# Gram inputs and key-query tiles in two transfers of 48 partitions each, in a delta-rule attention and two-MLP kernel

## The chip, the cores and the metric

The kernel runs on one core of a Trainium2 chip. The metric is the device time of one execution in microseconds (us); lower is better. The core has engines that work side by side, each through its own list of instructions in order: PE (matrix multiply; its weight loads are shown apart as PEld), DVE (vector), ACT (scalar functions), POOL (GpSimd) and SP, which here only issues transfers between HBM and on-chip memory. On-chip memory (SBUF) has 128 partitions.

## What is computed

A linear attention with a delta-rule state over 768 tokens for 4 x 8 heads of width 48, then an ELU MLP, then an MLP with a rational activation; cut from the reference:

```python
    k_n = k / (np.linalg.norm(k, axis=-1, keepdims=True) + 1e-06)
    for t in range(S):
        y[:, :, t] = np.einsum('bhd,bhde->bhe', q[:, :, t], state)
        v_old = np.einsum('bhde,bhd->bhe', state, kt)
        state = state + bt[:, :, :, None] * np.einsum('bhd,bhe->bhde', kt, vt - v_old)
...
    h = x @ w_in                                  # 3072 x 384 by 384 x 2048
    g = np.where(h > 0.0, h, alpha * (np.exp(np.minimum(h, 0.0)) - 1.0))
    return (g @ w_out).astype(np.float32)
...
    g = P / (Q + 1e-06)                           # second MLP: cubic over quadratic in h
    return (g @ w_out).astype(np.float32)
```

## The kernel before

The 768 tokens are cut into 12 chunks of 64 (`s`), two chunks to a window (`w`, six windows of 512 rows for the MLPs). A chunk's 32 heads lie in two halves (`hf`); in a half's tile, each of two heads-in-a-partition-column (`h`) has its 48 features at partitions 64h to 64h+47.

**Gram stage** (`g_item`): per chunk, two groups of 32 small matmuls (64 records in the trace, two for each) multiply keys by keys and queries. Its inputs are tiles of 128 x 1024 floats, `c_kg`, one for each chunk and half, loaded by `gin_ahead` into `wo`, `xg` or `gin` (the first six are parked in memory that other tiles use later; the name in the trace is that of the memory). `layout` on the host fills partitions 48 to 63 and 112 to 127 of these tiles with zeros; the matmuls read only the 48 rows of a head. **Solve stage** (`t_pieces`): the Gram blocks are transposed on DVE (`am<-gl_`) and a triangular system is inverted by a chain of DVE products and sums, in which ACT moves blocks (`tt<-tt`, `am<-tt`); it ends with the transpose `tp_t<-am`. **Chain stage** (`chain`): per chunk `ks`, two solves (`pa<-kv,tp_t` or `pa<-R,tp_t`), `lo`, `yy`, `xx`, `ku` on PE with DVE and ACT between them. It reads tiles `kq` (`c_kq`, the same shape and the same zero rows as `c_kg`) and `kv`. **MLP 1** (`H`, `A1`, `B1`, `C1`, `O`): matmuls of 512 columns, in groups of nine, between which the small groups of the next windows are put. **MLP 2** follows from about 560 us.

Weights arrive as 64-bit floats and are converted on ACT and DVE (`conv_x`, `conv_d`, `conv_s`; tiles `raw`, `ce`, `wo`, `wi`).

What sets the order: every operation is recorded first, and `order` plans all engines by a model of the chip (`simulate`, `backward`); ties and small shifts come from a table of random seeds (`MIX`), and `PUSH` gives the settings of successive passes, of which the best is kept. All instructions are then emitted at one line (L206). `gaps` puts dummy matmuls named `fill` (line 1629) in front of a small group where the plan leaves PE idle, only for groups planned after 20 us. SP issues its transfers in the order planned; eight completion semaphores are used in turn, so a transfer waits in SP's queue until the one eight before it has landed. `hold(t)` is a one-column copy on POOL into a tile that keeps its load from being issued before an event (the first mask, the first transpose); `follow(t, u)` does the same until tile `u` has landed.

At the start PE runs three warm-up matmuls on zeros (`pa<-tmp`), then four Gram groups for window 0. The first two use the first two `c_kg` tiles, the third and fourth the next two (`wo`, `xg`). Behind these in SP's queue are `mask_p`, `beta_l`, two `raw<-w_out`, two tiny coefficient loads, two `kv` and eight `wo<-w_in`; then, after the first transpose, the loads for window 1.

Of the kernel before, what the change touches and what calls it, by code (L numbers as in the profile page):

```python
# [20 lines left out]
D = 48  # L21
NSC = 12
# [164 lines left out]
class Recorder:  # L187
# [141 lines left out]
SLACK = {"small": 150, "F": 100, "x": 30, "issue": 450, "rate": 385, "land": 2300, "wait": 900, "space": 3500, "room": 264, "first": 460, "blk": 253.9, "use": 2250, "hold": 400, "jit": 300, "keep": 6000, "most": 5000, "step": 3500, "drift": 0,  "pj": 0}  # L329
MIX = [  # L330
# [4 lines left out]
]  # L335


PUSH = [(16000, 5000), (5000, 3000), (16000, 3000), (0, 3000), (20000, 3000), (13000, 3000), (0, 500), (18000, 3000)]


def draw(seed, n):
# [13 lines left out]
def order(ops):  # L355
# [30 lines left out]
    best = None  # L386
    for push, lead in PUSH:
        end = simulate(ops)
# [235 lines left out]
def kernel(  # L624
# [16 lines left out]
    rc = Recorder(nc)  # L641
    mm, act, vector, gpsimd = rc.mm, rc.act, Recorder.Eng(rc, "DVE", nc.vector), Recorder.Eng(rc, "POOL", nc.gpsimd)
# [74 lines left out]
    def hold(t):  # L717
        gpsimd.tensor_copy(out=t[:, 0, 0:1], in_=gate[-1])

    def follow(t, u):  # L720
        gpsimd.tensor_copy(out=t[:, 0, 0:1], in_=u[:, 0, 0:1])

    conv_q = []
    for f in range(NF):
# [82 lines left out]
    def gin_park(i):  # L807
        if i < 3:
            return wo1.rearrange("p f n -> p (f n)")[:, 1024 * i:1024 * i + 1024]
        if i == 3:  # L810
            t = ap1.tile([128, 3, 512], F32, tag="xs", name="xg")
        else:
            t = mp.tile([128, 3, 512], F32R, tag=("xh", "xl")[i - 4], name="xg", bufs=1).bitcast(F32)
        return t.rearrange("p c n -> p (c n)")[:, 0:1024]

    def gin_ahead(n):
        for _ in range(n):
            i = gin_n[0]
            if i == len(gin_q) or i >= 4 and len(gate) < 2:
                return  # L820
            park = i < 6
            if park or gin_l[0] < 2:
                w, s, hf = gin_q[i]
                if park:
                    t = gin_park(i)
                else:
                    t = ap2.tile([128, 1024], F32, tag="gin", name="gin", bufs=2)
                    gin_l[0] += 1
                t = t.rearrange("p (u n) -> p u n", u=8)
                if 4 <= i < 8:  # L830
                    hold(t)
                elif i >= 8 and hf:
                    follow(t, gin_t[s, 0][0])
                rc.dma(out=t, in_=c_kg[s, hf])
                gin_t[s, hf] = t, not park
                gin_n[0] += 1

# [4 lines left out]
    def ch_ahead(nm):  # L842
        if ch_n[nm] < len(ch_q):
            s, hf = ch_q[ch_n[nm]]
            if nm == "kq":
                t = ap2.tile([128, 8, 128], F32, tag="kq", name="kq")
                if s == 1:
                    hold(t)
                rc.dma(out=t, in_=c_kq[s, hf])
            else:  # L850
                if s == 1:
                    t = mp.tile([128, 2, DM], F32R, tag="wor", name="kv").bitcast(F32)
                    t = t.rearrange("p a b -> p (a b)").rearrange("p (u n) -> p u n", u=8)
                    hold(t)
                else:
                    t = ap2.tile([128, 8, 96], F32, tag="kv", name="kv")
                    if s == 0:
                        hold(t)
                rc.dma(out=t, in_=c_kv[s, hf])
            ch_t[nm, s, hf] = t  # L860
            ch_n[nm] += 1
# [33 lines left out]
    def g_item(j, s, bb):  # L895
# [31 lines left out]
        if bb:  # L927
            for hf in range(2):
                gin_l[0] -= gin_t.pop((s, hf))[1]
            gin_ahead(2)  # L930
# [139 lines left out]
    def chain(w, slots=SLOTS):  # L1070
# [14 lines left out]
        for j, s in enumerate(WINS[w]):  # L1085
# [75 lines left out]
            def yy(hfs, s=s, st=st):  # L1161
# [20 lines left out]
                for hf in hfs:  # L1182
                    if s > 0:
                        ch_ahead("kq")
# [299 lines left out]
    def early_loads():  # L1484
        gate.append(p_d[0][:, 0, 0:1])
        conv_loads(Q["wl"])
        for _ in range(2):
            ch_ahead("kv")
# [97 lines left out]
    for k in range(NP * NG2):  # L1586
        t = P + 2 * k
        if k < 2:
            t = T + (8.7, 15)[k]
# [30 lines left out]
    with tc.manual_schedule():  # L1620
        for o in first:
            i = idle.get(o, 0)
            for n in [2] * (i // 2) + [1] * (i % 2):
                if "w" not in wt:
# [5 lines left out]
                    out=wt["w"][:, 0:256 * n].rearrange("p (a b) -> p a b", a=k), lhsT=c,  # L1630
# [8 lines left out]
def layout(q, k, v, beta, moe_w_in, moe_w_out, moe2_w_in, moe2_w_out, moe2_a, moe2_b):  # L1639
    import numpy as np  # L1640

    f32 = np.float32
    B, H, S, Dh = q.shape
# [8 lines left out]

    def rows(k, q, cross):
        kq = np.concatenate([k, q], axis=-1).reshape(NSC, 2, 2, 2, Dh, 4, 128)
        o = np.zeros((NSC, 2, 2, 64, 8, 128), f32)
        for hf in range(2):
            for h in range(2):
                o[:, hf, h ^ (hf * cross), :Dh] = kq[:, hf, :, h].transpose(0, 2, 1, 3, 4).reshape(NSC, Dh, 8, 128)
        return o.reshape(NSC, 2, 128, 8, 128)

    kf, qf = feat(k), feat(q)
    c_kg = rows(kf, qf, 1)
    kf = kf.copy()
    kf[:, :, :, 1::2] = np.roll(kf[:, :, :, 1::2], 32, axis=-1)
    c_kq = rows(kf, qf, 0)
# [49 lines left out]
```

## Time and profile before

| what | us |
|---|---|
| three timed runs: median (lowest to highest) | 966.79 (965.37 to 967.17) |
| the profiled execution, own time | 966.62 |
| its span, first to last instruction | 964.8 |
| first 512-column matmul of MLP 1 | 69.12 |
| PE busy in the span | 943.4 |

How to read it: a window row gives a stretch (start:end, length), then for each engine busy time and, in brackets, the number of instructions, then the clock that PE was granted (1.00 is 2.4 GHz, 0.50 is 1.2 GHz), the busy share of the DMA engines and GB/s. A timeline row gives start, duration, engine, line, operation, out<-in, partitions and shapes, the count of merged instructions and, in square brackets, how long the engine sat idle before and what ended it ("issue": nothing that the profile shows). A row of waits gives who waited for whom: total us, times, longest. A queue row gives packets, MB and the share of 16 DMA engines; q1 carries the kernel's own transfers, q8 the code of PE. A landing row gives the time from a transfer's issue to its landing.

### The profile page before, as it was taken

The page shows a single profiled execution, that of the slowest core. Times are in us where ns is not written, and L with a number is a line of the kernel's source. Part 1 is how long each engine was busy: PE and PEld are TensorE (multiplying, and loading weights), DVE is VectorE, ACT ScalarE, POOL GpSimd, SP SyncE. Part 2 cuts the span into 40 slices and gives each one's busy share as a digit, 9 for nine tenths or more (in the row PEclk, how much of TensorE's full clock was granted, in tenths as well). Part 3 has the DMA queues.
Part 4 walks back from the last instruction along what each step waited for, and adds up shares of the span by engine and source line. Part 5 has one row for each costly group of instructions (what it writes and reads, how often), then busy time and mean ns, then how long its engine had stood idle before and what let it go on. Part 6 is the DMA issues. An engine that isn't in the chain of part 4 may idle for free.

```text
span 964.8 us, 24786 instructions
## 1 busy us (share of the span) xinstructions
PE 943.4 (98%) x10312; PEld 752.8 (78%) x10312; DVE 832.5 (86%) x1182; ACT 693.3 (72%) x1311; POOL 312.8 (32%) x227
## 2 busy tenths in 40 slices
PE   8789999999999999999999999999999999999997
PEld 4367777877778878887888888888888888888885
DVE  5899999998999888975645369999999999999997
ACT  5387899777878778778866666776776766766764
POOL 2100002423312322222222244363544643743432
PEclk9799999999999999999999999999999999999999
DMA  8364545234544455344529321020010010000000
GB/s 297 138 195 129 191 129 178 87 99 152 190 136 153 152 150 178 102 134 139 177 88 393 133 73 43 1 66 1 1 66 0 14 54 1 33 1 0 34 1 33
DMA packets 59521, 99.89 MB, mean 104 GB/s; under 512 B 6544, under 2 KB 39440, under 8 KB 59408
## 3 DMA queue, kind: packets, MB, share of 16 engines
q1 hardware_dynamic: 59408, 98.30, 31.1%
q8 instruction: 81, 1.33, 0.6%
q14 instruction: 32, 0.26, 0.1%
HBM read 76.25 MB, written 22.02 MB: 102 GB/s over the span
## 4 chain that ended last, share of the span: by engine, by line
PE 80%; DMA 3%; ACT 2%; DVE 2%; issue 0%; POOL 0%; ACTq 0%; SPq 0%; DVEq 0%; POOLq 0%
PE o L206 37%; PE h L206 16%; PE h_b L206 11%; PE h_a L206 10%; PE pa L206 7%; PE h_c L206 1%; DMA raw<-w_out 1%; DMA wo<-w_out 1%; ACT wo L206 1%; DVE wo L206 1%; DMA kv<-c_kv 1%; DMA gin<-c_kg 0%; ACT e L206 0%; ACT raw L206 0%; DVE gh L206 0%
## 5 line engine op out<-in xcount | busy, mean ns | idle before, releaser
L206 POOL TENSOR_TENSOR gl<-wo 128x1024 fp32r<-128x1024 f32 (+1 forms) x48 | 145.9, 3040 | 205.1 <-DVE wo L206 130.5
L206 PE MATMUL o<-gh,wor 128*128 128x512 f32 x576 | 198.1, 399 | 0.1
L206 PE MATMUL h<-xh,wi 128*128 128x512 f32 x546 | 186.2, 397 | 0.3 <-DVE e L206 0.3
L206 ACT ACTIVATE wo<-wo 128x1024 f32<-128x1024 f32 (+3 forms) x202 | 134.4, 698 | 61.8 <-DVE wo L206 55.8
L206 POOL TENSOR_TENSOR wor<-wo,wor 128x384 fp32r<-128x384 f32 x80 | 87.9, 1100 | 250.0 <-ACT wor L206 233.7
L206 PE MATMUL o<-gh,wo 128*128 128x512 f32 x576 | 138.5, 389 | 0.0
L206 PEld LDWEIGHTS o<-gh,wor 128*128 128x128 f32 x576 | 107.9, 188 | 25.4 <-DVE wor L206 0.7
L206 PEld LDWEIGHTS o<-gh,wo 128*128 128x128 f32 x576 | 108.1, 188 | 22.5
L206 PEld LDWEIGHTS h<-xh,wi 128*128 128x128 f32 x546 | 102.4, 188 | 24.5 <-issue 1.3
L206 PE MATMUL o<-gl,wor 128*128 128x512 f32 x288 | 112.4, 390 | 0.0
L206 PE MATMUL h<-xl,wi 128*128 128x512 f32 x273 | 106.6, 390 | 0.1
L206 DVE TENSOR_TENSOR gl<-e,gh 128x512 fp32r<-128x512 f32 x88 | 77.2, 878 | 26.0 <-ACT gh L206 25.1
L206 PE MATMUL h_b<-xh,wi 128*128 128x512 f32 x300 | 96.4, 389 | 0.0
L206 DVE SCALAR_TENSOR_TENSOR e<-e,h 128x512 f32<-128x512 f32 x91 | 62.3, 685 | 35.6 <-ACT e L206 34.3
L206 DVE SCALAR_TENSOR_TENSOR wo<-wo 128x1024 f32<-128x1024 f32 (+2 forms) x71 | 80.5, 1138 | 10.2 <-ACT wo L206 10.1
L206 PE MATMUL h_a<-xh,wi 128*128 128x512 f32 x276 | 88.8, 389 | 0.0
L206 ACT ACTIVATE e<-h 128x512 f32<-128x512 f32 x91 | 54.2, 596 | 29.2 <-PE h L206 28.5
L206 PE MATMUL o<-gl,wo 128*128 128x512 f32 x288 | 73.5, 390 | 1.2 <-POOL gl L206 0.7
L206 DVE SCALAR_TENSOR_TENSOR gh<-wo,ab_sb 128x1024 fp32r<-128x1024 f32 (+1 forms) x49 | 65.1, 1329 | 9.1 <-ACT wo L206 3.1
L206 ACT ACTIVATE gh<-e 128x512 fp32r<-128x512 f32 x96 | 60.0, 625 | 13.7 <-DVE e L206 8.2
L206 ACT ACTIVATE wor<-wo 128x384 fp32r<-128x384 f32 x96 | 49.8, 520 | 26.5 <-PE o L206 25.0
L206 ACT ACTIVATE wo<-h_b,ab_sb 128x1024 f32<-128x1024 f32 (+1 forms) x52 | 57.2, 1128 | 15.8 <-PE h_b L206 12.7
(176 smaller groups left out, 1802.1 us busy)
## 6 DMA issues: line engine op xcount, KB each, us to landing
kq<-c_kq SPq DMA_DIRECT2D x22, 512.0 KB, 5.3
kv<-c_kv SPq DMA_DIRECT2D x24, 384.0 KB, 5.0
gin<-c_kg SPq DMA_DIRECT2D x18, 512.0 KB, 4.0
raw<-w_out SPq DMA_DIRECT2D x42, 192.0 KB, 2.7
raw<-w_in SPq DMA_DIRECT2D x34, 192.0 KB, 3.1
o2d<-cs SPq DMA_DIRECT2D x32, 192.0 KB, 2.9
i2d<-cs SPq DMA_DIRECT2D x32, 192.0 KB, 2.5
wi<-i2d SPq DMA_DIRECT2D x16, 384.0 KB, 4.4
```

The costliest lines, as they stand in the source:

```text
L206: fn(**{k: v.real() if isinstance(v, View) else v for k, v in kw.items()})
```

## The change

Host side: `rows` packs `c_kg` and `c_kq` as 48 rows for each head instead of 64, without zeros: 384 KB a tile for 512 KB. Device side: each of the 24 `c_kg` and 22 loaded `c_kq` tiles is fetched by two transfers of 48 partitions, to partitions 0 to 47 and 64 to 111; partitions 48 to 63 and 112 to 127 are no longer written. `follow` makes two copies of 48 partitions, one for each transfer. `MIX` loses one seed and gains six others, and `PUSH` has other values, so the planned order changes throughout.

```diff
     def follow(t, u):
-        gpsimd.tensor_copy(out=t[:, 0, 0:1], in_=u[:, 0, 0:1])
+        for h in range(2):
+            r = slice(64 * h, 64 * h + D)
+            gpsimd.tensor_copy(out=t[r, 0, 0:1], in_=u[r, 0, 0:1])
...
-                rc.dma(out=t, in_=c_kg[s, hf])
+                for h in range(2):
+                    rc.dma(out=t[64 * h:64 * h + D], in_=c_kg[s, hf, h])
...
-                rc.dma(out=t, in_=c_kq[s, hf])
+                for h in range(2):
+                    rc.dma(out=t[64 * h:64 * h + D], in_=c_kq[s, hf, h])
...
-        o = np.zeros((NSC, 2, 2, 64, 8, 128), f32)
+        o = np.zeros((NSC, 2, 2, Dh, 8, 128), f32)
...
-PUSH = [(16000, 5000), (5000, 3000), (16000, 3000), (0, 3000), (20000, 3000), (13000, 3000), (0, 500), (18000, 3000)]
+PUSH = [(18000, 0), (6000, 0), (17000, 0), (0, 0), (19000, 0), (15000, 0), (0, 0), (17000, 0)]
```

SP's list from its first instruction, where it holds the loads for window 0 (`wo` and `xg` from `c_kg`), as a difference:

```order
-L1709 UNCONDITIONAL_BRANCH
-L206 DMA wo_91<-c_kg 128x1024 x2
+L1714 UNCONDITIONAL_BRANCH
+L206 DMA wo_91<-c_kg 48x1024 x4
 L206 DMA cm_sb<-mask_p 128x256
-L206 DMA wo_91<-c_kg 128x1024
-L206 DMA xg<-c_kg 128x1024
+L206 DMA xg<-c_kg 48x1024
+L206 DMA wo_91<-c_kg 48x1024 x2
+L206 DMA xg<-c_kg 48x1024
 L206 DMA bl<-beta_l 128x32
 L206 DMA raw<-w_out 128x384 x2
```

Four transfers became eight in front of `raw<-w_out`, and the fourth tile's halves stand around the third tile.

PE's list where the last Gram group of window 0 (`wo`, `xg` interleaved) meets the first of window 1 (`xg` alone), as a difference:

```order
 L206 MATMUL pa_83<-wo_91 32x2x32 x2
 L206 MATMUL pa_81<-xg 32x2x32 x2
-L1629 MATMUL fill<-cm_sb 128x512 x10
 L206 MATMUL pa_82<-xg 32x128 x2
 L206 MATMUL pa_83<-xg 32x128 x2
```

The ten dummy matmuls between the two are gone; the eight and a half in front of the first solve stay, and between the groups of window 1 there are four where two stood.

ACT's list in the solve of window 0, around the block moves `tt<-tt` and `am<-tt` (`gl`, `p`: results of the Gram groups of window 1; `wo`: a weight tile from `w_out`), before:

```order
L206 ACTIVATE gl__425<-pa_82 128x256
L206 ACTIVATE p<-pa_82 128x256
L206 ACTIVATE tt<-tt 128x16x16
L206 ACTIVATE gl__425<-pa_83 128x256
L206 ACTIVATE p<-pa_83 128x256
L206 ACTIVATE am<-tt 128x16x16 x2
```

and after the change:

```order
L206 ACTIVATE gl__426<-pa_82 128x256
L206 ACTIVATE p<-pa_82 128x256
L206 ACTIVATE wo_91<-wo_91 128x192
L206 ACTIVATE tt<-tt 128x16x16
L206 ACTIVATE am<-tt 128x16x16 x2
L206 ACTIVATE p<-pa_83 128x256
```

A conversion of a weight tile, which waits for a `wo<-w_out` transfer, now stands ahead of the block move.

## Rows read from the trace of the kernel before

**Rows 1.** The page, part 1: busy time, share of span, instructions.

```profile
PE 943.4 (98%) x10312; PEld 752.8 (78%) x10312; DVE 832.5 (86%) x1182; ACT 693.3 (72%) x1311; POOL 312.8 (32%) x227
```

**Rows 2.** Windows: MLP 1 with the later chains, and MLP 2.

```profile
69.12:560.00 490.88, 488.25 (x7200) 390.78 (x7200) 402.44 (x760) 381.02 (x901) 116.29 (x115) 1.00 0.48 154
560.00:964.80 404.80, 399.07 (x1759) 329.48 (x1757) 377.26 (x297) 274.05 (x283) 186.07 (x81) 1.00 0.07 24
```

**Rows 3.** Waits of PE from 69.12 us to the end.

```profile
PE pa L206 <- DVE R L206: 1.3, 5, 0.3
PE o L206 <- POOL gl L206: 0.7, 1, 0.7
...
PE pa L206 <- DMA gin<-c_kg: 0.2, 1, 0.2
```

**Rows 4.** Timeline of PE, first 22 us.

```profile
1.45 5.49 PE L206 MATMUL pa<-tmp 128*128 128x512 f32 x6 [1.45 <-DVE tmp L288]
6.87 1.02 PE L206 MATMUL pa<-wo 48*32 48x128 f32 x61
...
9.49 0.30 PE L206 MATMUL gp<-xg 48*32 48x128 f32 x2 [0.38 <-DMA xg<-c_kg]
...
12.48 0.24 PE L206 MATMUL pa<-wo 48*32 48x64 f32 x2 [1.45 <-issue]
...
13.06 8.85 PE L1629 MATMUL fill<-cm_sb 128*128 128x512 f32 x20
```

**Rows 5.** Windows over the first loads: the last number is GB/s.

```profile
3.00:5.50 2.50, 2.50 (x4) 1.01 (x3) 0.00 (x0) 0.00 (x0) 0.00 (x0) 1.00 1.05 406
...
7.70:9.00 1.30, 1.30 (x88) 1.15 (x67) 0.77 (x3) 0.49 (x2) 0.46 (x4) 1.00 1.04 365
9.00:9.80 0.80, 0.42 (x25) 0.31 (x30) 0.74 (x2) 0.58 (x3) 0.79 (x7) 1.00 0.77 182
```

**Rows 6.** Landings of the first two c_kg transfers, issued at 0.74 and 1.18.

```profile
DMA to landing us min/median/max: 3.6/3.6/3.6
...
DMA to landing us min/median/max: 4.5/4.5/4.5
```

**Rows 7.** DMA queues from 7.7 to 9.8 us, then from 9.8 to 10.0.

```profile
q1 hardware_dynamic: 701, 0.62, 93.5%
...
q8 instruction: 1, 0.02, 32.3%
```

**Rows 8.** Timeline of DVE in the solve of window 0.

```profile
14.55 2.00 DVE L206 STREAM_TRANSPOSE am<-gl__175 128x1024 f32<-128x1024 f32 x1 [0.45 <-ACT gl__175 L206]
...
35.59 0.42 DVE L206 TENSOR_TENSOR tmp<-tt 128x256 f32<-128x256 f32 x1 [0.52 <-DVE tt L206]
...
42.54 1.97 DVE L206 STREAM_TRANSPOSE tp_t<-am 128x1024 f32<-128x1024 f32 x1
```

**Rows 9.** Timeline of PE from 22 to 46 us.

```profile
22.46 1.14 PE L206 MATMUL pa<-xg 48*32 48x128 f32 x64 [0.55 <-DMA xg<-c_kg]
...
35.13 10.45 PE L1629 MATMUL fill<-tt,cm_sb 128*128 128x512 f32 x18 [4.05 <-DVE tt L206]
45.50 0.88 PE L206 MATMUL pa<-kv,tp_t 32*32 32x48 f32 x64
```

**Rows 10.** Windows from 31 to 45.5 us: PE idle, then dummy matmuls.

```profile
31.08:35.13 4.05, 0.00 (x1) 0.00 (x1) 3.75 (x6) 1.72 (x6) 1.45 (x2) 0.50 0.42 129
35.13:40.96 5.83, 5.83 (x7) 2.49 (x8) 5.17 (x7) 0.00 (x0) 0.00 (x0) 0.50 0.26 91
40.96:45.50 4.54, 4.54 (x12) 1.90 (x10) 4.37 (x6) 0.36 (x1) 0.00 (x0) 1.00 0.00 0
```

**Rows 11.** Timeline: the w_out load on SP, the conversion on ACT.

```profile
22.39 0.33 SPq L206 DMA_DIRECT2D wo<-w_out  x1
...
31.30 0.65 ACT L206 ACTIVATE wo<-wo 128x192 f32<-128x192 f32 x2 [0.53 <-DMA wo<-w_out]
```

More of the change, by code (lines that the diff above doesn't have):

```diff
@@ L1654, in rows @@
         kq = np.concatenate([k, q], axis=-1).reshape(NSC, 2, 2, 2, Dh, 4, 128)
-        o = np.zeros((NSC, 2, 2, 64, 8, 128), f32)
+        o = np.zeros((NSC, 2, 2, Dh, 8, 128), f32)
         for hf in range(2):
             for h in range(2):
-                o[:, hf, h ^ (hf * cross), :Dh] = kq[:, hf, :, h].transpose(0, 2, 1, 3, 4).reshape(NSC, Dh, 8, 128)
-        return o.reshape(NSC, 2, 128, 8, 128)
+                o[:, hf, h ^ (hf * cross)] = kq[:, hf, :, h].transpose(0, 2, 1, 3, 4).reshape(NSC, Dh, 8, 128)
+        return o
     kf, qf = feat(k), feat(q)
```

7 rows, old and new, of the table MIX are left out of this document.

## The prediction

> **What bounds the kernel now.** I read the page first, then windows by stage, then PE's waits, and only then the timelines of the first 70 us. PE is busy for 943.4 of 964.8 us [rows 1]; DVE's 832.5 us are the next longest. The windows say where PE's idle time lies: from the first 512-column matmul at 69.12 us to 560 us it is busy for 488.25 of 490.88 us, and in MLP 2 for 399.07 of 404.80 [rows 2]. The waits in this stretch are small: 1.3 us in five pieces on DVE, 0.7 us near the end on POOL, and a single one of 0.2 us on a transfer that the change touches, `gin<-c_kg` [rows 3]. So after 69 us the time is the sum of PE's matmuls, and their number does not change. What a transfer can give or cost is in the first 69 us, where engines wait for each other in one line: the `c_kg` loads, four Gram groups on PE, the DVE transposition and solve (14.55 to 44.51 us), and then the chain of window 0.
>
> The profiled execution took 966.62 us, its span and 1.82 us around it. The median of the three runs is 0.17 us above. I sum against 966.62 and leave that difference out. A measurement of this kernel can tell about 0.2%, 1.93 us, from no change.
>
> **The change, part by part.** *Bytes at the start.* The first four tiles are four transfers of 512 KB; they become eight of 192 KB, 512 KB less in all. The stream runs at 406 GB/s from 3.0 to 5.5 us and at 365 from 7.7 to 9.0 [rows 5]; by their middle, 385, the 512 KB are 1.36 us. The first two landings, at 0.74 + 3.6 and 1.18 + 4.5, lie 1.3 us apart [rows 6], which is the same rate. SP issues one every 0.44 us [rows 6], so the eight and the mask are out by 4.7 us, ahead of the stream.
>
> *What waits for them.* Not the first group: PE is in its warm-up matmuls from 1.45 to 6.94 us, and the first group starts at 6.87 [rows 4], more than a microsecond after the second tile landed at 5.7. The third group waits 0.38 us for its tile until 9.49. In the middle of the fourth, PE stops for 1.45 us until 12.48 with no producer shown [rows 4]. That is missing code: no packet of PE's code queue runs from 7.7 to 9.8 us, and one runs in 9.8 to 10.0 [rows 7], just as the transfers' rate has fallen from 365 to 182 GB/s [rows 5]. So what the fourth group waits for is a code packet that starts when the bulk loads thin out. With 512 KB less they thin out 1.36 us earlier. The bounds are 0 (the packet's start has another cause) and 1.83 us (both waits, 1.45 + 0.38, vanish). I take 1.1 us, nearer to 1.36 than to 0, since some of the saved bytes fall into the first microseconds, when the stream is only starting. The transpose at 14.55 us [rows 8] then starts at 13.45.
>
> The Trainium skill, DMA: Bandwidth & Descriptors, section Queues, rings and completion order, has each DMA engine take turns between its queues packet by packet; by that, code would not stand behind the bulk loads and this term would be 0. The packet's start above speaks against it; a rival below prices it.
>
> *The solve.* It is 30 us of DVE back to back, 14.55 to 44.51, and moves as one piece unless ACT is late. ACT's block move `tt<-tt` now stands behind a conversion that needs the `wo<-w_out` transfer. That transfer is issued at 22.39 and its conversion starts at 31.30 [rows 11], held up by six `c_kg` and `c_kq` tiles and two `kv` in front of it. Those six become 768 KB smaller, 2.0 us by the same rate. The first user of the block move is the DVE product at 35.59 [rows 8]. Even at 31.3 us, with the 0.38 us conversion and the 0.65 us move, ACT is done at 32.3, 2.2 us ahead of that product at its new 34.5. Cost 0; the cover is those 2 us, and if the six tiles took 2 us longer instead, it would be gone.
>
> *The dummy matmuls.* The ten that go ran from 13.06 to 21.9 us [rows 4] and held nothing up; the next group waited for its tile until 22.46 [rows 9]. Without them PE idles there and may be granted the low clock for window 1's Gram groups. In the one rise that the trace shows, PE had been busy for 5.83 us at 0.50 [rows 10]; such a stretch costs 2.9 us, and two additional dummies between these groups 0.9 each. These 4.7 us stand against the 4.05 that PE idles before the next dummies [rows 9] and tiles that land a good microsecond earlier. Cost 0. If the clock stayed low throughout, the four groups (1.1 us each), four dummies and the wait for code between them would need some 17.7 us for the 12.7 between 22.46 and 35.13, and the solve would be up to 5 us late.
>
> The other dummies matter. They start at 35.13 when the DVE row before 35.59 is done, run at a granted clock of 0.50 until 40.96 and at 1.00 after [rows 10], and end at about 45.5. The first solve on PE starts at 45.50 [rows 9], though `tp_t` is ready at 42.54 + 1.97 = 44.51 [rows 8]. So PE's own filling makes the chain 0.9 us late. (At 1.00 twenty records took 8.85 us [rows 4]; the eighteen here, two of them half as wide, need 7.5 us at that speed and took 10.45.) Moved 1.1 us forward, the dummies end between 45.0 (the clock rises at the same moment as before) and 43.5 or earlier (it rises earlier, and `tp_t`, at 43.4, gates). The first solve moves by 0.5 to 2.0 us. I take 1.8, near the upper end, because only the low-clock stretch makes the dummies the later of the two.
>
> *Chain and MLP 1.* From 45.5 us all three engines wait on each other step by step, so the 1.8 us pass on. Later `gin` and `kq` tiles gain a shorter transfer and lose SP issue slots (46 more) and eight more copies on POOL; PE's only wait on them is the 0.2 us above. I take 0.1. PE's list from the first 512-column matmul on has the same matmuls, in 77 uninterrupted runs of them instead of 78: nothing that I would price. The new order can add or remove waits like the 1.3 us on DVE [rows 3]; bounds plus and minus 2 us, taken as 0.
>
> Sum: 966.6 - 1.8 - 0.1 = 964.7 us, 0.20% less.
>
> **Rivals.** *The code packet does not move* (or the dummies' clock rises at the old moment): the first solve gains 0 to 0.5 us, the time is 966.3. For it: the page gives no cause for the wait. Against it: where the packet stands in the rate's fall.
>
> *Half-tile transfers are slower a byte.* All transfers in this trace go to 128 partitions, so no row shows it. If two halves took 1.33 x 1.25 = 1.67 us for the 1.33 of a whole tile, the fourth tile would be 1.4 us late. The packet and the transpose would follow, the dummies too, and half of it would be lost behind them: + 0.7, 967.3 us. The Trainium skill, SBUF — State Buffer, sections Door 1: The DMA port swizzle and "Can I just issue two DMAs to hit both halves?", speaks for this: partitions 0 to 63 reach 8 of 16 ports (196 GB/s for 328 at 1 MiB), and two transfers to the two halves run one after the other. An estimate from its figures, 393 KB at 196/328 of the rate, is those 1.67 us. No run here shows it.
>
> *The same at its bound, slower than before:* each half takes as long as a whole tile took, 1.33 us. The four additional ones put the fourth tile 5.3 us later, at 14.8. The fourth group's code is there by then, so the transpose is 3.7 us late, the first solve 2.8 to 3.8: 970 us. It decides from 2.8 us of delay on (0.9 are behind the dummies), that is from 2.0 us a tile instead of 1.33.
>
> *The order:* the same gain at the start, but waits on DVE in MLP 1, where it is busy for 402 of 491 us [rows 2], grow or shrink: 961.7 to 968.
>
> *The change doesn't do what it says:* SP's list has the eight transfers of 48 partitions; this I leave out.
>
> **How the numbers follow.** The forecast has 50%: of that 28 faster by over 0.2%, 21 within, 1 slower, since its centre stands on the edge and its own range is 962.5 to 966.3. The code packet that does not move: 18% (3, 14, 1). Halves slower by a quarter: 14% (0, 11, 3). Their bound, or a low clock that stays: 6%, all slower. The order: 12% (6, 2, 4). Together 37% faster, 48% within, 15% slower. The range 961.5 to 968.5 takes in all but the bound of the halves, part of the order's tails, and the forecast's last tenth below.
>
> **What would show it.** Right: the stop in the fourth Gram group shrinks or ends near 11.4 us, `am<-gl_` starts at about 13.5, `tp_t` ends at about 43.4, the first solve starts right behind it, and the first 512-column matmul at about 67.3. Wrong: `am<-gl_` at 14.5 or later (then look at the third group's wait for `xg` and at GB/s between 3 and 9 us); the dummies still the last before the first solve; ACT's block move after 34 us; or a first 512-column matmul near 67.3 and yet the same span, with more PE waits after 69 us. The last would mean that the order gave back what the start won.

## The result: 1% slower

The changed kernel takes 976.67 us (median of four runs, 974.70 to 977.24) where the kernel before takes 966.93; the ratio is 1.0101, with a 95% interval from 1.0083 to 1.0118. The profiled execution took 977.24 us, the longest of the four; its span is 975.3. Four runs in a slower state (one of e7 and one of e14 below, two of the kernel before) are left out of all medians and costs. The prediction said 964.7 and a range of 961.5 to 968.5, so it was wrong, and in sign.

| where | before | after | later by |
|---|---|---|---|
| transpose `am<-gl_` starts (DVE) | 14.55 | 17.36 | 2.8 |
| `tp_t<-am` ends (DVE) | 44.51 | 48.81 | 4.3 |
| first solve (PE) | 45.50 | 52.48 | 7.0 |
| first 512-column matmul (PE) | 69.12 | 78.70 | 9.6 |
| end of the span | 964.8 | 975.3 | 10.5 |

After the first 512-column matmul only 0.9 us is added. The page shows nearly the same sums of work as [rows 1]; DVE has 8 us more. The kernel's own transfers moved 92.27 MB for 98.30 before: the 6.03 MB of zero rows are gone. Page of after, part 1, and the row of these transfers (packets, MB, share of 16 DMA engines):

```profile
PE 943.1 (97%) x10296; PEld 753.9 (77%) x10296; DVE 840.6 (86%) x1182; ACT 692.8 (71%) x1311; POOL 319.1 (33%) x235
...
q1 hardware_dynamic: 58672, 92.27, 32.1%
```

*The first loads.* Windows of after over the stretches of [rows 5]; the last number is GB/s, the one ahead the busy share of the DMA engines:

```profile
3.00:5.50 2.50, 2.50 (x4) 1.01 (x3) 0.00 (x0) 0.00 (x0) 0.00 (x0) 1.00 1.04 175
...
7.70:9.00 1.30, 1.30 (x94) 1.20 (x88) 0.71 (x2) 0.42 (x2) 0.22 (x2) 1.00 1.00 158
```

The DMA engines are as busy as before, but move 175 and 158 GB/s where they moved 406 and 365. The last half of the fourth tile, issued at 4.4 us, took 7.5 us to land, which is at 11.95:

```profile
L206 SPq DMA_DIRECT2D xg<-c_kg x1: 421/421/421, 4.4 to 4.4; - x1
...
DMA to landing us min/median/max: 7.5/7.5/7.5
```

PE's timeline, first 16 us, answers to [rows 4]: three waits for halves and the stop for code that was there before.

```profile
9.91 0.40 PE L206 MATMUL gp<-wo 48*32 48x128 f32 x2 [0.74 <-DMA wo<-c_kg]
...
11.10 0.40 PE L206 MATMUL gp<-wo 48*32 48x128 f32 x2 [0.79 <-DMA wo<-c_kg]
...
11.99 0.30 PE L206 MATMUL gp<-xg 48*32 48x128 f32 x2 [0.49 <-DMA xg<-c_kg]
...
14.95 0.32 PE L206 MATMUL pa<-wo 48*32 48x64 f32 x2 [1.19 <-issue]
```

*The stretch of window 1.* PE's timeline of after from 24 to 53 us, beside [rows 9]:

```profile
24.23 0.60 PE L206 MATMUL pa<-xg 48*32 48x128 f32 x2 [8.20 <-DMA xg<-c_kg]
...
29.29 2.93 PE L1634 MATMUL fill<-cm_sb 128*128 128x512 f32 x4
32.15 0.88 PE L206 MATMUL pa<-xg 48*32 48x128 f32 x20
36.53 1.28 PE L206 MATMUL pa<-xg 48*32 48x128 f32 x44 [3.50 <-issue]
...
40.43 3.65 PE L1634 MATMUL fill<-cm_sb 128*128 128x512 f32 x4
44.01 1.05 PE L206 MATMUL pa<-gin 48*32 48x128 f32 x64
44.99 7.57 PE L1634 MATMUL fill<-tt,cm_sb 128*128 128x512 f32 x18
52.48 0.71 PE L206 MATMUL pa<-kv,tp_t 32*32 32x48 f32 x48
```

Before, the four Gram groups were done at 31.1 us and PE waited for DVE [rows 9]. Now the last group starts at 44.01; the eighteen dummies stand behind it in PE's list and end when the first solve starts. The time went in four pieces: PE idles 8.20 us until the first `xg` half has landed, and 2.3 us more for the other halves; it stops for 3.50 us with no producer shown; it runs at the low clock until 43.81; and the dummies come last. PE's waits of after from 17 to 53 us, then windows, clock behind the busy times:

```profile
PE pa L206 <- DMA xg<-c_kg: 10.5, 3, 8.2
```

```profile
13.09:43.81 30.72, 15.49 (x272) 8.24 (x251) 24.19 (x50) 14.47 (x53) 5.10 (x13) 0.50 0.77 181
43.81:52.48 8.67, 8.67 (x83) 4.16 (x82) 7.72 (x10) 1.57 (x5) 0.67 (x3) 1.00 0.43 113
```

The stop of 3.50 us is for code. From 22 to 34.1 us the DMA queues show no packet of q8; from 34.1 to 34.3 us they show one:

```profile
q1 hardware_dynamic: 25, 0.07, 88.4%
q8 instruction: 1, 0.02, 34.0%
```

DVE's solve was held up as well, by ACT, whose block move stood behind evacuations of PE's stopped group and the weight conversion. Timelines of ACT and DVE, beside [rows 8] and [rows 11]:

```profile
37.88 0.38 ACT L206 ACTIVATE gl__426<-pa 128x256 f32<-128x256 f32 x1 [7.23 <-PE pa L206]
...
38.95 0.40 ACT L206 ACTIVATE wo<-wo 128x192 f32<-128x192 f32 x1
39.22 0.65 ACT L206 ACTIVATE tt<-tt 128x256 f32<-128x256 f32 x1
```

```profile
17.36 1.95 DVE L206 STREAM_TRANSPOSE am<-gl__179 128x1024 f32<-128x1024 f32 x1 [0.45 <-ACT gl__179 L206]
...
39.91 0.42 DVE L206 TENSOR_TENSOR tmp<-tt 128x256 f32<-128x256 f32 x1 [2.16 <-ACT tt L206]
...
46.86 1.95 DVE L206 STREAM_TRANSPOSE tp_t<-am 128x1024 f32<-128x1024 f32 x1
```

*The chain* took 26.22 us, from 52.48 to 78.70, where it took 23.62. PE's stops for code in it before, then after, and a window of after:

```profile
53.07 0.66 PE L206 MATMUL y<-ub,p 64*64 64x48 f32 x26 [0.54 <-issue]
...
65.44 0.27 PE L206 MATMUL y<-s_st,kq 48*64 48x48 f32 x5 [1.45 <-issue]
```

```profile
60.67 0.37 PE L206 MATMUL y<-ub,p 64*64 64x48 f32 x10 [0.92 <-issue]
...
69.76 0.45 PE L206 MATMUL pa<-R,tp_t 32*32 32x48 f32 x23 [0.66 <-issue]
...
73.76 0.56 PE L206 MATMUL y<-ub,p 64*64 64x48 f32 x23 [1.66 <-issue]
```

```profile
74.53:77.95 3.42, 3.42 (x72) 2.75 (x72) 1.13 (x3) 1.70 (x5) 0.00 (x0) 0.50 1.02 199
```

A packet of q8 starts 2.3 to 2.9 us ahead of the end of each stop. The stops are 3.2 us instead of 2.0, and behind the last one PE ran 3.4 us at the low clock.

### The profile page after: what moved, and what is told of

It reads as the page before. It is cut to its first block, busy times and chain, and to the rows that moved or that the text cites. A ratio compares the mean times of both kernels' runs of the same rounds, so it can differ in the third digit from the quotient of the medians.

```text
span 975.3 us, 24853 instructions
## 1 busy us (share of the span) xinstructions
PE 943.1 (97%) x10296; PEld 753.9 (77%) x10296; DVE 840.6 (86%) x1182; ACT 692.8 (71%) x1311; POOL 319.1 (33%) x235
## 3 DMA queue, kind: packets, MB, share of 16 engines
q1 hardware_dynamic: 58672, 92.27, 32.1%
## 4 chain that ended last, share of the span: by engine, by line
PE 49%; DVE 1%; DMA 1%; ACT 0%; issue 0%; ACTq 0%; DVEq 0%
PE o L206 24%; PE h_b L206 10%; PE h_a L206 10%; PE h L206 4%; PE h_c L206 1%; DVE wo L206 1%; PE pa L206 1%; DMA raw<-w_in 1%; ACT wo L206 0%; DVE gh L206 0%; DVE s_st L206 0%; DVE gl L206 0%; ACT raw L206 0%; ACTq L1714 0%; DVE ce L206 0%
## 5 line engine op out<-in xcount | busy, mean ns | idle before, releaser
L206 PEld LDWEIGHTS h<-xh,wi 128*128 128x128 f32 x546 | 102.4, 188 | 25.4 <-issue 1.1
L206 DVE TENSOR_TENSOR gl<-e,gh 128x512 fp32r<-128x512 f32 x88 | 79.4, 902 | 30.7 <-ACT gh L206 29.5
```

The source lines that it names most:

```text
L206: fn(**{k: v.real() if isinstance(v, View) else v for k, v in kw.items()})
```

## Experiments

Each kernel was timed against the kernel before on the same chip; its cost is the ratio times 966.9 us, less 966.9. "Old order" means that every engine's list is that of the kernel before, "new order" that of the changed kernel: the planner still sees the transfers of its own kernel, and only what is emitted for one differs (with the copies of `follow` on POOL that belong to it). "Halves" are two transfers of 48 partitions for each `c_kg` and `c_kq` tile, "whole" one of 128.

| kernel | median us | cost us (95%) | transpose | first solve | first 512-col. |
|---|---|---|---|---|---|
| changed kernel (new order, halves) | 976.67 | +9.8 (8.0 to 11.4) | 17.36 | 52.48 | 78.70 |
| e1: old order, halves | 969.14 | +2.1 (0.9 to 3.5) | 16.28 | 47.51 | 71.53 |
| e2: new order, whole | 968.41 | +1.4 (0.0 to 2.7) | 15.53 | 45.38 | 69.54 |
| e3: old order, 2 of 128 x 512 | 968.85 | +2.2 (1.0 to 3.5) | 15.33 | 45.83 | 70.40 |
| e4: old order, 2 of 64 partitions | 980.08 | +13.1 (9.5 to 16.7) | 18.11 | 48.75 | 73.71 |
| e9: old order, 1 of 112 partitions | 968.10 | +0.8 (-0.5 to 2.0) | 15.73 | 46.77 | 70.99 |
| e7: new order, first four whole | 973.32 | +6.8 (4.5 to 9.1) | 14.57 | 49.76 | 73.39 |
| e8: new order, only first four halved | 971.21 | +3.1 (1.5 to 4.8) | 17.88 | 47.64 | 71.84 |
| e14: new order, windows 0 and 1 whole | 969.40 | +1.4 (-0.3 to 3.1) | 13.94 | 44.16 | 68.34 |
| e5: new order, halves, ten dummies back | 974.59 | +7.4 (5.2 to 9.7) | 18.40 | 51.88 | 75.02 |
| e10: e5 and the block move ahead | 974.39 | +7.3 (5.1 to 9.4) | 17.07 | 50.28 | 73.76 |
| e13: fewer dummies before first solve | 975.23 | +8.0 (5.8 to 10.2) | 17.87 | 50.36 | 78.16 |
| e11: three kq halves held back | 976.40 | +9.0 (6.7 to 11.3) | 18.39 | 51.81 | 78.46 |
| e15: e10, kq half and dummies as in e1 | 974.19 | +7.1 (4.6 to 9.4) | 17.62 | 50.03 | 76.07 |
| e17: e1 without the ten dummies | 971.96 | +4.8 (3.1 to 6.6) | 15.76 | 48.80 | 74.50 |
| e18: before without the ten dummies | 968.07 | +1.5 (0.3 to 2.7) | 14.55 | 44.71 | 68.45 |
| e12: before, more dummies | 971.45 | +4.9 (3.1 to 6.7) | 13.72 | 46.22 | 73.53 |
| e16: before, fewer dummies | 967.69 | +0.5 (-1.0 to 2.0) | 14.00 | 44.14 | 69.52 |

The last three columns are of one profiled execution each, in us from its start. They scatter by some tenths of a us: in the four kernels with whole tiles and the old order, whose first loads are the same, the first tile landed between 4.22 (e18) and 4.37 us (before). Two costs with these intervals differ clearly only from about 2 to 3 us on.

The theories: that the halves move bytes at half the rate (T), that the new order does the damage (O), or that the number of transfers does (N).

### The transfers or the order: e1 to e4

e1, old order (`out` is the tile, `in_` the packed half-tiles):

```diff
-        self.add("SP", self.nc.sync.dma_start, dict(out=out, in_=in_), [out], [in_], SLACK["issue"], 2000, n)
+        fn = self.nc.sync.dma_start
+        if cut:
+            def fn(out, in_):
+                for h in range(2):
+                    self.nc.sync.dma_start(out=out[64 * h:64 * h + D], in_=in_[h])
...
```

> The order of the kernel before on every engine, dummies included; only each c_kg and c_kq transfer becomes two of 48 partitions (and the gin copies on POOL two each). Theory T (a 48-partition transfer moves bytes at about half the rate, so tiles land late): the transpose am<-gl_ starts near 17.4 us as in the changed kernel, the first solve is 3 to 5 us late, total 970 to 973. Rival O (the new order does the damage, the transfers are harmless): 966 to 968. Rival N (it is the number of transfers, with eight in flight, not their partitions): 970 to 973 too, told apart by the run with two transfers of 128 x 512.

e2, new order, with padded tiles; the first half's instruction loads the tile and the second's nothing:

```diff
-        self.add("SP", self.nc.sync.dma_start, dict(out=out, in_=in_), [out], [in_], SLACK["issue"], 2000, n)
+        fn = self.nc.sync.dma_start
...
+            def fn(out, in_):
+                if (v.base, v.ids.min()) not in self.half:
+                    self.half.add((v.base, v.ids.min()))
+                    self.nc.sync.dma_start(out=full.real(), in_=in_)
...
```

> The order of the changed kernel on every engine, without the ten dummies, but each c_kg and c_kq tile is one transfer of 128 partitions with its zero rows again. T: tiles land as before, the transpose starts near 14.5 us; what is left is what the order itself costs, 0 to 3 us: 966 to 970. O: 975 to 977, as the changed kernel. N: as T.

e3 and e4, old order, with padded tiles, in the place of e1's line:

```diff
+    self.nc.sync.dma_start(out=out[:, 4 * h:4 * h + 4], in_=in_[:, 4 * h:4 * h + 4])
```

> The order of the kernel before; each c_kg and c_kq tile in two transfers of 128 partitions x 512 columns, 256 KB each, same bytes as before. T: each half takes 0.65 to 0.7 us behind the other, tiles land within 0.5 us of before, total 966.5 to 968. N: as the run with 48 partitions, 970 to 973. O: 967.

```diff
+    self.nc.sync.dma_start(out=out[64 * h:64 * h + 64], in_=in_[64 * h:64 * h + 64])
```

> The order of the kernel before; each c_kg and c_kq tile in two transfers of 64 partitions x 1024 columns, 256 KB each, same bytes as before. T: each half takes about 1.35 us behind the other (half the rate), the fourth tile is later still than with 48 partitions, by 4 x 0.5 us; total 972 to 976. N: as the run with 128 x 512. O: 967.

Windows from 6 to 9 us, in which only these loads and the mask run: kernel before, e1, e3, e4.

```profile
6.00:9.00 3.00, 3.00 (x134) 1.98 (x132) 0.77 (x3) 0.80 (x3) 0.46 (x4) 1.00 1.00 382
```

```profile
6.00:9.00 3.00, 2.94 (x132) 2.07 (x130) 0.82 (x3) 0.85 (x3) 0.51 (x5) 1.00 1.09 221
```

```profile
6.00:9.00 3.00, 2.68 (x134) 1.98 (x132) 1.20 (x4) 1.02 (x3) 0.86 (x8) 1.00 1.02 357
```

```profile
6.00:9.00 3.00, 1.30 (x66) 1.03 (x69) 0.00 (x0) 0.31 (x1) 0.00 (x0) 0.88 1.07 240
```

Two transfers over all partitions run at 357 GB/s, nearly as one does; two of 64 or 48 partitions at 240 and 221. So for the rate it is the partitions and not the number of transfers, and T has it about right (0.58 of 382): a half tile of 192 KB lands 0.9 to 1.1 us behind the one ahead of it in e1, a half of 64 partitions about 1.15. A quarter of the bytes less shortens a half by some 0.15 us. The Trainium skill, SBUF — State Buffer, section Door 1: The DMA port swizzle, has partitions 0 to 63 reach half of the ports, and 64 to 127 the other half; the trace agrees (240 of 382 GB/s, 0.63). In the time, however, each theory missed at least once. Halves alone cost 2.1 us and not 3 to 6, the order alone 1.4, and both together 9.8. The two interact, and the next runs look for how. e3 costs 2.2 us with its loads nearly in time; of this its profile shows 0.3 at the first solve, the rest later, and what causes that stays open. By the time alone e1 and e3 can't be told apart, so the number of transfers may have a share in e1's 2.1 us; the first solve, 2.0 us late in e1 and 0.3 in e3, speaks for the partitions. e4 costs far more than e1 in the same order, and more than T's 972 to 976: its profile is 4.6 us late at the first 512-column matmul and loses 5.0 more behind it, where PE waits 2.6 us for DVE `R` (1.3 before) and 1.4 for `gin` and `kq` loads (0.2 before). Nor does the order alone cost its 1.4 us at the start: e2's profile, the longest of its ten runs, has the first solve 0.1 us early, the first 512-column matmul 0.4 late, and 3.6 us more behind that.

### Which loads: e7, e8, e14

All have the new order; `whole` decides what is emitted for a tile (e7: `i < 4`; e8: `i >= 4` and every kq tile; e14: `i < 8` and kq of chunk 1).

```diff
-rc.dma(out=t[64 * h:64 * h + D], in_=c_kg[s, hf, h])
+rc.dma(out=t[64 * h:64 * h + D], in_=c_kg[s, hf], part=h, whole=i < 4)
```

> The changed kernel, order the same on every engine, but the first four c_kg tiles (window 0) are one transfer of 128 partitions each; all later ones stay two of 48. Theory S (the delay begins with these four): the transpose starts at 14.5 to 15.5 us instead of 17.4 and all behind it moves, total 968 to 971. Rival W (the tiles of window 1 are what counts): first solve still after 50 us, total 973.5 to 976.

> The converse: order of the changed kernel, the first four c_kg tiles in two transfers of 48 partitions each, all later c_kg and c_kq tiles whole. S: the transpose at 17 us, total 973.5 to 976. W: the transpose at 17 us too, but window 1's groups are in time, first solve at 47 to 48.5, total 969 to 971.

> The changed kernel, same order on every engine; the c_kg tiles of windows 0 and 1 (the first eight) and the kq tiles of chunk 1 are whole transfers of 128 partitions, all later c_kg and c_kq tiles stay two of 48. If only the loads ahead of the first 512-column matmul count: first solve near 45.5 us, total 967.5 to 969.5, as with all tiles whole (968.4). If the later halves cost as well (bus or SP): 970 to 973.

W was nearer. With the first four whole the cost falls by 3.0 us (9.8 to 6.8, just beyond the intervals), with all the others whole by 6.7 (to 3.1), and with both by 8.4 (to 1.4 in e2). e14, in which every tile after window 1 is still halved, is where e2 is. So the loss comes from eight `c_kg` and two `c_kq` tiles in the first 40 us; the 36 tiles that are still halved in e14 cost nothing that these runs can tell.

### Code packets and dummies: e5, e17, e18, e11

e5 puts the ten dummies back into the new order:

```diff
-            if idle > 430 and o.start > 20000:
+            if idle > 430 and o.start > 12000:
```

> The changed kernel with one thing put back: the ten dummy matmuls between the last Gram group of window 0 and the first of window 1 (order and transfers of the changed kernel otherwise). Theory C (late tiles leave PE idle without dummies, so window 1's Gram groups and the dummies behind them run at the low clock, and that is what makes the first solve wait for PE): PE holds the high clock for most of 16 to 45 us, the first solve comes at 48.5 to 50 us instead of 52.5, total 971 to 973.5. Rival L (the tiles and code of window 1 arrive too late at any clock): first solve 51.5 or later, 975 to 977.

e17 and e18 take them out of the old order, with halves and with whole tiles:

```diff
     idle = gaps(first)
+    del idle[next(o for o in first if o in idle)]
```

> The old order with all c_kg and c_kq tiles in halves (969.1 so far, 1.0022 of before), without the ten dummies between the Gram groups of window 0 and 1. Theory K (the dummies carry PE past a code boundary before the loads of window 1 begin, and hold the clock): without them the code packet that came at 17 us comes at about 33, PE stops in the second Gram group of window 1, runs at the low clock from 13 to past 40 us, the first solve is at 49.5 to 51 instead of 47.5, total 971.5 to 974. Rival (the dummies do not matter, something else in the order does): 968.5 to 970.

> The kernel before, whole tiles, without the ten dummies. Theory K: the code packet comes about 9 us behind the first load of window 1, near 27, with time in hand; first solve at 45 to 46, total 966.5 to 968.5. If the clock alone decided: first solve 1 to 3 us late, total 968.5 to 970.

PE's timelines of e18, e17 and e5:

```profile
22.30 1.70 PE L206 MATMUL pa<-xg 48*32 48x128 f32 x64 [9.18 <-DMA xg<-c_kg]
...
28.43 1.22 PE L206 MATMUL pa<-xg 48*32 48x128 f32 x42 [1.61 <-issue]
...
35.08 8.89 PE L1630 MATMUL fill<-tt,cm_sb 128*128 128x512 f32 x18
44.71 1.09 PE L206 MATMUL pa<-kv,tp_t 32*32 32x48 f32 x64 [0.74 <-DVE ce L206]
```

```profile
23.79 0.60 PE L206 MATMUL pa<-xg 48*32 48x128 f32 x2 [9.37 <-DMA xg<-c_kg]
...
33.34 1.22 PE L206 MATMUL pa<-xg 48*32 48x128 f32 x42 [4.08 <-issue]
...
39.87 8.99 PE L1643 MATMUL fill<-tt,cm_sb 128*128 128x512 f32 x18
48.80 0.88 PE L206 MATMUL pa<-kv,tp_t 32*32 32x48 f32 x64
```

```profile
39.57 0.30 PE L206 MATMUL pa<-gin 48*32 48x64 f32 x3 [3.62 <-issue]
...
44.38 7.57 PE L1634 MATMUL fill<-tt,cm_sb 128*128 128x512 f32 x18
51.88 0.88 PE L206 MATMUL pa<-kv,tp_t 32*32 32x48 f32 x64
```

Without dummies the clock is low in both e17 and e18 for most of 12 to 42 us and of 14 to 38 us. With whole tiles that does no harm to the first solve: the code packet starts at 26.10 us, 8.8 us behind the first `xg` issue (17.30), the stop is 1.61 us, and the solve waits for DVE. With halves the packet starts at 30.81, 12.3 us behind the first issue (18.50), the stop is 4.08 us, and PE's dummies are the last link. The dummies are worth 2.7 us with halves (4.8 less 2.1) and 1.5 with whole tiles by the times, two figures that the intervals don't separate; the profiles do: without dummies the first 512-column matmul is 3.0 us later with halves and 0.7 earlier with whole tiles. So K holds for the place of the packet and the stop, and e17 falls into its range; that halves make the dummies worth more is shown by one profile of each. In e5, in the new order, they were worth 2.4 (9.8 less 7.4), within the intervals and less than C said: one packet came early (17.96 us), but the next one fell into the loads (36.69) and PE stopped three records ahead of the end of the third group. The first solve gained only 0.6 us, as L said; the other 3.1 up to the first 512-column matmul were gained in the chain, which neither theory looked at.

No trace shows when a packet is asked for, but all of them bear on it. With the ten dummies it starts while these run (15.20 us before, 17.03 in e1, 17.96 in e5). Without them it never starts in the 8 to 9 us in which PE stands still, but only after PE's first matmul of window 1: 3.8 us after it in e18 and 4.7 to 4.8 in e2, e8 and e14, where the tiles in flight are whole, and 7.0 us after it in e17 and 8.5 to 10.2 in the changed kernel, e7, e11 and e13, where they are halves. So PE's own progress has to come first, and then the loads in flight hold the packet up, halves for longer; e17 and e18 have the same lists and differ in the transfers alone. The other packets fit. Counted from the first `xg` issue, the packet in window 1 starts 9.2 us later in e2 and e8, where these tiles are whole, and 14.1 and 14.4 us later in the changed kernel and e7, where they are halves. e11 tests it by holding the three kq halves (`late`) back behind the DVE result `red` and the w_out load:

```diff
+    for o in late:
+        first.remove(o)
+    i = 1 + max(first.index(red), first.index(loads[b]))
+    first[i:i] = late
...
+            if o is late[0]:
+                nc.gpsimd.tensor_copy(out=v.real()[:, 0, 0:1], in_=u[:, 0:1])
```

> The changed kernel with the three half-tile kq loads behind the gin loads held back until a DVE result at about 33 us (one more one-column copy on POOL), and behind the w_out load. Theory Q (PE's code packet, at 34.2 us in the changed kernel, comes only when the bulk loads in flight thin out): the code packet comes 2 to 3 us earlier, PE's stop of 3.5 us in window 1's second Gram group shrinks to under 1.5, w_out lands near 35 instead of 38.4, the first solve comes 2 to 3 us earlier: total 973.5 to 975. If the packet has another cause, it stays at 34 and the total at 976 to 977.

The packet came 12.5 us behind the first issue instead of 14.1, PE's stop shrank to 2.60 us, and w_out landed at 36.1 instead of 38.4. This is the direction of Q, but its sizes were missed: the packet started 0.6 us earlier in the profile instead of 2 to 3, the stop should have been under 1.5 us, and the time, 976.40, is in the rival's range; the 0.8 us are within the intervals. Three kq halves were not what the packet waited for most.

### What is last before the first solve: e10, e13, e15

e10 is e5 with ACT's three block moves put right behind what they need:

```diff
+    i = next(i for i, o in enumerate(acts) if o.tag[0] == "tt<-tt" and o.tag[1] == 256)
+    for o in acts[i:i + 3]:
+        first.remove(o)
+        first.insert(1 + max(first.index(d) for d in o.deps), o)
```

> The changed kernel with the ten dummies put back (974.6 so far) and, besides, ACT's block move tt<-tt, am<-tt moved in ACT's list ahead of the evacuations and the weight conversion that it stood behind (in the run with the dummies alone the conversion waited for w_out until 40.8 us). Theory P (PE's list is the last link: its Gram groups, then eighteen dummies, then the first solve): tp_t ends 4 to 6 us earlier, near 45, but the first solve stays where PE's dummies end, total 973.5 to 975. Rival A (ACT's order is what makes the solve late): total 969.5 to 972.

e13, at the dummies that wait for DVE ahead of the first solve:

```diff
+            if o.wait is not None:
+                i //= 2
```

> The changed kernel with eight records of dummies (four matmuls) instead of eighteen ahead of the first solve. P: they end about 48.5 us, the first solve starts right behind tp_t near 49 instead of 52.5, total 973 to 974. If tp_t or something else were the last link: first solve still at 52, total 976.7; if the clock falls for want of dummies, the chain gives it back: 975 to 977.

e15 is e10 with the first kq half (`k`) behind the gin loads, and one short dummy instead of two long ones:

```diff
+    first.remove(k)
+    first.insert(first.index(gin) + 1, k)
+    idle[few[-1]] = 1
```

> The changed kernel, all tiles in halves, with the ten dummies back, ACT's block move ahead, the first kq half behind the gin loads in SP's queue instead of ahead of the xg loads, and one short dummy instead of two long ones between window 1's last two Gram groups. If these make up what the new order pays more for halves than the old one: first solve at 47.5 to 48.8 us, total 970 to 972 (old order with halves 969.1, plus the 1.5 of the new order with whole tiles). If something else in the order does: 973.5 to 975.

DVE's timeline of e10, and PE's:

```profile
45.07 1.99 DVE L206 STREAM_TRANSPOSE tp_t<-am 128x1024 f32<-128x1024 f32 x1
```

```profile
42.78 7.57 PE L1639 MATMUL fill<-tt,cm_sb 128*128 128x512 f32 x18
50.28 0.88 PE L206 MATMUL pa<-kv,tp_t 32*32 32x48 f32 x64
```

With ACT's block move ahead, `tp_t` is ready 3.2 us before the first solve, and the time stays where e5 had it (974.4 and 974.6). P holds: PE's list is the last link, and ACT's order is not. In e13 the dummies end earlier and the first solve starts right behind `tp_t` (50.21), as P said, but the chain then took 27.8 us, and the total gains 1.8 us of the 3 to 4, within the intervals. That is the range of e13's third reading, in which the chain gives the gain back. e15 was to bring together what I took for all of the difference to e1. It fell short: 7.1 us against the 2.1 of e1. Its profile shows where part of the rest lies. PE's timeline of e15 and a window:

```profile
36.49 0.42 PE L206 MATMUL pa<-gin 48*32 48x64 f32 x3 [3.94 <-issue]
...
40.70 9.40 PE L1646 MATMUL fill<-tt,cm_sb 128*128 128x512 f32 x18
```

```profile
71.74:75.15 3.41, 3.41 (x71) 2.71 (x72) 1.64 (x4) 1.50 (x5) 0.00 (x0) 0.50 1.04 198
```

Against e1 the transpose is 1.3 us later, the eighteen dummies take 9.40 us for 8.28, and the chain is 2.0 us longer, with a stretch at the low clock as in the changed kernel. Which feature of the new order decides this is not settled.

### Fewer and more dummies in the kernel before: e12, e16

Both edits stand where the dummies ahead of the first solve are emitted; e12 first, with matmuls that do not wait:

```diff
+            if o.wait is not None and i:
+                for _ in range(8):
+                    nc.tensor.matmul(
...
```

> The kernel before, whole tiles, with sixteen more records of dummies (eight matmuls) in the 4 us in which PE waited ahead of the eighteen before the first solve, so that the clock does not fall there. If the first solve is late only because those eighteen ran at the low clock: they end at 42.8 us, the first solve starts behind tp_t at 44.6 instead of 45.5, total 965.8 to 966.4 against 966.7. If not, no change.

```diff
+            if o.wait is not None and i:
+                i -= 4
```

> The kernel before, whole tiles, with fourteen instead of eighteen records of dummies (two matmuls fewer) ahead of the first solve. If they are the last link there: they end 1.7 us earlier, the first solve starts behind tp_t at 44.7 instead of 45.5, and the total is 0.5 to 0.9 us less than before, unless PE's code in the chain stage falls elsewhere (plus or minus 2).

e12 was mis-sized: sixteen records take 7.1 us and not the 4 that were free, so the dummies again ended last, at 46.2 us, and the chain grew to 27.3 us. In e16 the first solve starts right behind `tp_t` (44.14 behind 43.88), as the prediction's reading of that place says, but the chain grew from 23.6 to 25.4 us and the time is the same. Neither beats the kernel before, and no other kernel here does.

## Why the prediction was wrong

**The bytes.** The step that failed first is the rate. The prediction said that all rows are of transfers to 128 partitions, and took their 385 GB/s for the halves all the same. It measured 175 GB/s from 3.0 to 5.5 us, and a tile took 2.1 to 2.2 us instead of the 1.0 that 384 KB would have taken. The term for the start was -1.1 us and measured +2.8, at the transpose. The rival "at its bound" named the point from which it decides, 2.0 us a tile, and that is where the tiles came to lie; it had 6%, together with a low clock that stays, and its 970 us was still 6.7 too little. The estimate of 1.67 us from the figures of the Trainium skill, SBUF — State Buffer, section Door 1: The DMA port swizzle, was too low. It was scaled down with the bytes, and 48 partitions gain little over 64 (0.9 to 1.1 us a half in e1 for 1.15 in e4).

**The code packet.** That it starts when the bulk loads thin out was right for the first loads: the packet moved with them, from 9.90 to 12.43 us, and the last half landed at 11.95. The rule of the Trainium skill, DMA: Bandwidth & Descriptors, section Queues, rings and completion order, by which queues take turns packet by packet, does not show in the starts: 9 us behind the first load of window 1 with whole tiles, 12 to 15 with halves.

**The cover of ACT's block move.** "If the six tiles took 2 us longer instead, it would be gone" is what happened: w_out landed 7.1 us later, at 38.36, and DVE waited 2.16 us instead of 0.52. The condition was right and was not carried on from the rival, which gave each tile 1.33 us more, 8 us for six. But w_out did not end ACT's wait here: ACT waited 7.23 us for PE's stopped group until 37.88, and the conversion at 38.95 followed without a wait. The prediction left this evacuation, ahead of the block move in ACT's list, out of its working. e10 shows, moreover, that DVE's wait was not the last link.

**The ten dummies.** "Cost 0" was nearly right for whole tiles up to the first solve (e18: 0.8 us earlier in the profile; by the time 1.5 us, 0.3 to 2.7) and wrong for halves, where their loss costs 2.7 us (e17) or about 2.4 (e5, within the intervals). The prediction had them hold the clock only. They also carried PE past a code boundary between two bursts of loads: before, the next code packet after that of 9.9 us came at 15.2, and in the changed kernel at 34.16. The working for a clock that stays low (17.7 us for four groups, dummies and code, a solve up to 5 us late) was the better forecast, and stood as an aside.

**The first solve.** -1.8 us became +7.0. That PE's own dummies end last there was right (e13, e16).

**The chain.** "The 1.8 us pass on" missed 2.6 us more: 1.2 us more of stops for code, and the 3.4 us at the low clock. This is seen in one profile of each kernel; e7, with the same order, has a chain of 23.63 us. Why it falls on some kernels and not on others was not isolated.

**After 69 us** -0.1, with 2 us either way, fits the profile of the changed kernel: +0.9; and e14's time shows no price for later halves. But the same order has 3.6 us more than before behind the first 512-column matmul in e2 and 4.5 in e14, in one long execution each. So these two profiles put the small cost of the order alone there and not in the first 69 us, and the plus and minus 2 us may be too narrow. (The order's rival, 961.7 to 968, is wider than the 2 us it comes from; the prediction does not say by what.)

**The range** failed since each rival stood alone. One cause, the rate, made the first tiles late, took away ACT's cover, kept PE idle without its dummies, and held the code back. Of the 9.8 us, the halves in the old order give 2.1, the missing dummies with halves about 2.5, and the new order with whole tiles 1.4, part of which may be the dummies again (each known to 1.3 to 3 us); about 4 us of the interaction stay without a cause that these runs isolate. That the late halves are what starts it is shown, since with whole tiles the same order costs 1.4; which feature of the order makes them cost 9.8 and not 2.1 stays open.

## What to carry to other kernels

A transfer to half of the partitions is priced by a row of such a transfer, or by half the rate; leaving out bytes by leaving out partitions can make it longer. Where one unknown price stands under several covers, work the pessimistic value through all of them together, as one rival. Dummy matmuls can also decide when the next code is fetched, as the ten did here, so taking some away can move the stops for code behind them.

## What the runs showed of the hardware

One transfer of 112 partitions, 448 KB, landed later than one of 128 with 512 KB. The edit of e9, which has the old order:

```diff
-        self.add("SP", self.nc.sync.dma_start, dict(out=out, in_=in_), [out], [in_], SLACK["issue"], 2000, n)
+        fn = self.nc.sync.dma_start
+        if cut:
+            def fn(out, in_):
+                self.nc.sync.dma_start(out=out[0:64 + D], in_=in_[0:64 + D])
...
```

> The order of the kernel before, each c_kg and c_kq tile in one transfer of 112 partitions (0 to 111), 448 KB instead of 512: only the upper zero rows are left out. By bytes the first tiles land 1.17 us apart instead of 1.33 and the fourth 0.6 us earlier: total 965.5 to 966.5. If a transfer lasts as long as its fullest path, however few rows the others carry, they land 1.33 us apart as before: 966.5 to 967.5.

Windows from 6 to 9 us of e9 and of e7, whose first four tiles are whole, on the same chip:

```profile
6.00:9.00 3.00, 2.30 (x128) 1.77 (x125) 0.89 (x3) 0.91 (x3) 0.57 (x5) 1.00 1.03 261
```

```profile
6.00:9.00 3.00, 2.88 (x130) 1.79 (x128) 0.82 (x3) 0.84 (x3) 0.51 (x5) 1.00 1.01 387
```

261 GB/s for 387: the last two tiles landed 1.52 us apart in e9 and 1.36 in e7. Both expectations, 1.17 and 1.33, were too low, and no run tells why. In the time e9 is not told from the kernel before (+0.8, -0.5 to 2.0).
